# An S5 scan and a Mish layer on one core: both rotation products in one instruction, two reordered steps, one snapshot on VectorE, a shorter quarter-wise stage

## The chip, the cores and the metric

One core of a Trainium2 chip runs the whole kernel. The metric is the device time of one execution in microseconds (us); the runs shown are three executions of the kernel before, and their median is the time to be compared. TensorE does the matrix products, VectorE and ScalarE the elementwise work, GpSimd and SyncE mostly issue DMAs. Each engine works through its own queue in order; semaphores order the engines among each other.

## The reference

x has 2048 rows of 1024 (one batch). Types are bf16.

```
xn  = (x - mean) / sqrt(var + 1e-5)                       # per row
A:  Lam_bar = exp(dt * Lam);  B_bar = ((Lam_bar - 1) / Lam) * (B_re + i B_im)
    Bu = xn @ B_bar^T                                      # 2048 x 1024, complex
    h[t] = Lam_bar * h[t-1] + Bu[t]                        # along the rows
    A = 2 * Re(h @ (C_re + i C_im)^T) + xn * Dskip
B:  g = xn @ w1 + b1                                       # 1024 -> 3584
    B = (g * tanh(softplus(g))) @ w2                       # Mish, 3584 -> 1024
out = x + A + B
```

## The kernel before

The 2048 rows are worked on in four blocks of 512, counted from 0 as the variable `blk` does. Each block has the same stages on TensorE: the w1 product (Mish follows on ScalarE), the B product (the two parts of Bu), the w2 product, and the C product, which adds to the same eight PSUM banks as w2's; bank u holds quarter u // 2 of the block's rows and half u % 2 of the columns. `finish` then adds a quarter's two banks to x on VectorE (L1525) and ScalarE's queue stores the sum.

**The scan.** The complex recurrence is turned into two real ones: `recur` runs a real scan for each part (L1354, part "A") and rotates by tables of sine and cosine before and behind it. A rotation ("turn") takes the two parts of one row of 128 states, multiplies both by one table and then both by the other (two products into `mt`), and then forms a sum and a difference of those. It stands at three places: in `project_in` (block 0, read from PSUM), in `rotate_in` (before the scan of blocks 1 to 3) and in part "B" of `recur` (behind the scan). Eight rows j make the states; `hT` holds them, and later the C product's operands.

**Products with fewer multiplications.** From block 1 on the B product, and in blocks 2 and 3 w1's too, are done by a Strassen-Winograd scheme: seven products (numbered 1 to 7) of half size, whose PSUM banks are chained. In `w_product` a quad (letters p, q, s, w, x, y, z) opens bank X with product 1 and adds 6, 7 and 4 to it one after the other; bank Y holds product 2, bank Z products 5 and 3. Between two that chain on one bank, `w_evacuate` reads what is there: after 1, 5 and 6 a "snapshot" to SBUF (`snap`, L1004 on ScalarE or L1007 on VectorE, two instructions each), after 2, 3 and 7 a "join" of a bank and a snapshot (L1021, VectorE), after 4 a plain copy. So product 7 waits for the snapshot behind 6, and product 4 for the join behind 7.

**The order** is written out by hand in strings: `STEPS` for block 2, `LAST` for block 3. In them `p1` is product 1 of quad p with its evacuation, `a`..`d` are the B product's pairs, `r3` is rotate_in of row 3, `u0` the opening products of w2 on bank 0 (`open_unit`, the first six tiles f, from three ring slots), `g2` a Mish over a group of tiles (ScalarE), `h8` a scaling of a w2 row (ScalarE; each fourth also issues three stores on GpSimd's queue), `k0` one pending VectorE step (a sum of weights, L1134 or L1189, and a store on GpSimd's queue), `M1` a load on ScalarE's queue, `A0` and `B0` parts "A" and "B" of the scan of row 0, `S0` a few small VectorE instructions. What stands left to right is the order of each engine's own queue.

**Weights** stream through a ring of seven slots of 512 KB. SyncE issues the load of a slot as soon as TensorE has told that the slot's last user is done (`item_done`); the same SyncE queue carries the transposing DMAs of the next block's `xnT`.

**The tail.** In `tail` the last `njt` rows of the C product are done quarter by quarter (row j, part ci, then the quarter's two banks), so that `finish` of one quarter runs beside the next one's products; the other rows are done for all eight banks. `njt` is 1 in block 0 and 3 in blocks 1 to 3. The slots of the quarter-wise rows are given back behind the last quarter.

Of the kernel before, what the change touches and what calls it, by code (L numbers as in the profile page):

```python
# [5 lines left out]
ALU = mybir.AluOpType  # L6
# [3 lines left out]
P = 128  # L10
# [153 lines left out]
def build_kernel(nc, A_x, A_Lambda_re, A_Lambda_im, A_B_re, A_B_im, A_C_re, A_C_im,  # L164
# [5 lines left out]
    TB = 512  # L170
    NB = S // TB
# [14 lines left out]
             " d4 u6 r2 u4 n0 r3 r4 k0 k0 r5 k0 k0 n1 r6 r7")  # L186
    STEPS = ("p1 p5 p2 q1 q5 k0 k0 p6 q2 s1 k0 p7 s5 p3 k0 q6 s2 k0 p4 q7 k0 q3 k0 s6 q4 k0 m3 k0 g0 a2 a1 k0 s7 s3 k0 b2 b1 k0 s4 g1 m2 a5 "
            "b5 a6 b6 a3 b3 a7 b7 c2 d2 a4 b4 c5 c1 d5 d1 h12 r0 c6 c3 h13 d6 d3 h14 c7 h15 w1 d7 r1 w5 w2 l0 c4 d4 w6 x1 x5 x2 k0 w7 k0 w3 r2 "
            "x6 w4 y1 y5 y2 k0 k0 x7 x3 y6 A0 x4 z1 z5 g2 h8 h9 h10 M1 z2 B0 y7 h11 y3 z6 y4 u0 z7 u2 r7 z3 u1 z4 u7 r3 g3 r4 r6 r5")
    LAST = ("p1 p5 p2 q1 q5 p6 S0 q2 s1 p7 s5 p3 q6 s2 M4 p4 q7 q3 k0 k0 s6 q4 g0 a2 a1 k0 s7 k0 s3 m6 b2 b1 s4 G1 G0 g1 a5 G3 b5 G2 a6 b6 "  # L190
# [11 lines left out]
    VE = Queue(nc, "ve")  # L202
    AC = Queue(nc, "ac")
# [3 lines left out]
    def sb(name, shape, dtype):  # L207
        return nc.alloc_sbuf_tensor(name, shape, dtype)
# [17 lines left out]
    hT = sb("hT", [P, 2, NJ, TB], bf16)  # L226
    b_hT = [[Buf("hT%d_%d" % (ci, j)) for j in range(NJ)] for ci in range(2)]
# [3 lines left out]
    tab = sb("tab", [P, 2, NJ, TB], bf16)  # L231
    b_tab = [Buf("tab%d" % j) for j in range(NJ)]
# [6 lines left out]
    mt = sb("mt", [P, 2, 2, TB], bf16)  # L239
    b_m = [Buf("m%d" % i) for i in range(2)]  # L240
# [29 lines left out]
    def cj(n, j):  # L270
        return cs[:, CN.index(n), j:j + 1]

    ps = nc.alloc_psum_tensor("ps", [P, 8, TB], f32)
    b_ps = [Buf("ps%d" % i) for i in range(8)]
# [7 lines left out]
    hT16 = nc.alloc_sbuf_tensor_at("hT16", [P, 2, NJ, TB], f16, offset=base_h)  # L282
# [19 lines left out]
    def wsm(n, lo, hi):  # L302
        return cs[:, CN.index("den") + n, lo:hi]
# [71 lines left out]
    vop, aop, pop = VE.op, AC.op, PO.op  # L375
# [221 lines left out]
    def b1(f):  # L597
        return par[:, 3 * NJ + f:3 * NJ + f + 1]
# [88 lines left out]
    for f in range(4):  # L687
        first_raw(f, 0, NK // 2)
    PE.op(lambda e: e.transpose(ps16(6)[:, 0:NST], st[:, :], ident[0:NST, 0:NST]),
          reads=[b_st, b_ident], writes=[b_ps[6]])  # L690
# [184 lines left out]
    def banks_of(j):  # L875
        return 2 * ((j + 2) % 4)

    def rotate_in(j):
        for s in range(2):
            vop(lambda e, s=s: e.tensor_tensor(  # L880
                mt[:, s, :, :], hT16[:, :, j, :], tab[:, s, j, :].unsqueeze(1).to_broadcast([P, 2, TB]), op=ALU.mult),
                reads=[b_hT[0][j], b_hT[1][j], b_tab[j]], writes=[b_m[s]])
        vop(lambda e: e.tensor_tensor(hT[:, 0, j, :], mt[:, 0, 0, :], mt[:, 1, 1, :], op=ALU.add),
            reads=b_m, writes=[b_hT[0][j]])
        vop(lambda e: e.tensor_tensor(hT[:, 1, j, :], mt[:, 0, 1, :], mt[:, 1, 0, :], op=ALU.subtract),
            reads=b_m, writes=[b_hT[1][j]])
# [73 lines left out]
    def w_out(i, ci):  # L960
        f0 = 4 * i + 2 * ci
        return f0, *places(SPLIT[0], f0, 2)
# [27 lines left out]
    def w_evacuate(blk, i, n, keep):  # L990
        X, Y, Z = W_BANKS[i]
        at = REAL[i]
        ig = wsm(3, at, at + 1)
        b_ig = b_wsm[3][at]

        def bank(b):
            return ps[:, b, :].rearrange("p (j t) -> p j t", j=2)

        def whole(dst, b_dst, b, ci, queue):
            f0 = 4 * at + 2 * ci  # L1000
            for j in range(2):
                o, p = dst[:, j, :], ps[:, b, j * TH:(j + 1) * TH]
                if queue is AC:
                    aop(lambda e, o=o, p=p, j=j: e.activation(o, p, AF.Identity, scale=ig, bias=b1(f0 + j)),  # L1004
                        reads=[b_ps[b], b_par, b_ig], writes=b_dst)
                else:
                    vop(lambda e, o=o, p=p, j=j: e.tensor_scalar(o, p, ig, b1(f0 + j), op0=ALU.mult, op1=ALU.add),  # L1007
                        reads=[b_ps[b], b_par, b_ig], writes=b_dst)

        def snap(b, ci, queue):  # L1010
            k = free_snaps.pop(0)
            dst = snaps[:, 2 * k:2 * k + 2, D - TH:D]
            whole(dst, [b_snap[k]], b, ci, queue)
            return dst, k

        def join(b, kept, ci, th):
            src, k = kept
            free_snaps.append(k)
            f0, dst, b_dst = w_out(i, ci)
            dst = dst[:, :, th * TH:(th + 1) * TH]  # L1020
            vop(lambda e: e.scalar_tensor_tensor(out=dst, in0=bank(b), scalar=ig, in1=src, op0=ALU.mult, op1=ALU.add),  # L1021
                reads=[b_ps[b], b_snap[k], b_ig], writes=b_dst)

        if n == 1:
            keep["w", i, "a"] = snap(X, 0, AC)
        if n == 2:
            join(Y, keep["w", i, "a"], 0, 0)
        if n == 5:
            keep["w", i, "e"] = snap(Z, 1, AC)
        if n == 6:  # L1030
            keep["w", i, "v"] = snap(X, 0, VE if i == 6 else AC)
        if n == 3:
            join(Z, keep["w", i, "v"], 0, 1)
        if n == 7:
            join(X, keep["w", i, "e"], 1, 1)
        if n == 4:
            f0, dst, b_dst = w_out(i, 1)
            whole(dst[:, :, 0:TH], b_dst, X, 1, AC if i in (0, 1, 3, 4) else VE)
# [289 lines left out]
    def project_in():  # L1328
        for j in range(NJ):
            if j:  # L1330
                row_sizes(0, j - 1)
            bank = banks_of(j)
            for ci in range(2):
                for k in range(NK):
                    PE.mm(lambda e, j=j, ci=ci, k=k, bank=bank: e.matmul(  # L1335
                        ps[:, bank + ci, :], lhsT=BT[:, ci, j, k, :], rhs=xnT[:, k, :], start=k == 0, stop=k == NK - 1),
                        reads=[b_BT[j]] + b_xnT, writes=[b_ps[bank + ci]], first=k == 0, last=k == NK - 1)
            u = ps[:, bank:bank + 2, :]
            for s in range(2):
                vop(lambda e, s=s, u=u, j=j: e.tensor_tensor(  # L1340
                    mt[:, s, :, :], u, tab[:, s, j, :].unsqueeze(1).to_broadcast([P, 2, TB]), op=ALU.mult),
                    reads=[b_ps[bank], b_ps[bank + 1], b_tab[j]], writes=[b_m[s]])
            vop(lambda e, j=j: e.tensor_tensor(hT[:, 0, j, :], mt[:, 0, 0, :], mt[:, 1, 1, :], op=ALU.add),
                reads=b_m, writes=[b_hT[0][j]])
            vop(lambda e, j=j: e.tensor_tensor(hT[:, 1, j, :], mt[:, 0, 1, :], mt[:, 1, 0, :], op=ALU.subtract),
                reads=b_m, writes=[b_hT[1][j]])
            if j < 7:
                transpose_C(2 * j + 2)
                transpose_C(2 * j + 3)

    def recur(blk, j, parts="AB"):
        for ci in range(2 if "A" in parts else 0):
            init = 0.0 if blk == 0 else qi[:, ci, j:j + 1]
            vop(lambda e, ci=ci, init=init: e.tensor_tensor_scan(  # L1354
                out=hT[:, ci, j, :], data0=cj("r", j).to_broadcast([P, TB]), data1=hT[:, ci, j, :], initial=init,
                op0=ALU.mult, op1=ALU.add),
                reads=[b_hT[ci][j], b_cs["r"]] + ([b_qi] if blk else []), writes=[b_hT[ci][j]])
        if "B" not in parts:
            return
        for s in range(2):  # L1360
            vop(lambda e, s=s: e.tensor_tensor(  # L1361
                mt[:, s, :, :], hT[:, :, j, :], tab[:, s, j, :].unsqueeze(1).to_broadcast([P, 2, TB]), op=ALU.mult),
                reads=[b_hT[0][j], b_hT[1][j], b_tab[j]], writes=[b_m[s]])
        vop(lambda e: e.tensor_tensor(hT[:, 0, j, :], mt[:, 0, 0, :], mt[:, 1, 1, :], op=ALU.subtract),
            reads=b_m, writes=[b_hT[0][j]])
        vop(lambda e: e.tensor_tensor(hT[:, 1, j, :], mt[:, 0, 1, :], mt[:, 1, 0, :], op=ALU.add),
            reads=b_m, writes=[b_hT[1][j]])
        if blk == NB - 1:
            aop(lambda e: e.activation(hT[:, :, j, :], hT[:, :, j, :], AF.Copy, scale=wz[:, 2:3]),
                reads=[b_hT[0][j], b_hT[1][j], b_wz[2]], writes=[b_hT[0][j], b_hT[1][j]])  # L1370
# [17 lines left out]
    def tail(blk, base):  # L1388
# [38 lines left out]
                                     start=st_, stop=last),  # L1427
                  reads=[b_hT[ci][j], b_c], writes=[b_ps[bank]], first=st_, last=last)

        njt = 1 if blk == 0 else 3  # L1430

        X, Y, Z, W = (0, 2), (4, 6), (5, 7), (1, 3)
        BANKS = {1: X, 6: X, 4: X, 2: Y, 5: Z, 3: Z, 7: W}
# [72 lines left out]
        i = blk % 2  # L1506
# [22 lines left out]
        if ends:  # L1529
            for m, q0, h in ((0, 0, 0), (1, 0, 1), (2, 2, 0), (3, 2, 1)):  # L1530
# [3 lines left out]
                    reads=[b_KS[m]] + b_x, writes=[b_KS[m]])  # L1534
            tmp, b_tmp = KS[:, 3, 1, :], b_KS[3]
            vop(lambda e: e.scalar_tensor_tensor(out=tmp, in0=ps[:, 7, :], scalar=wz[:, 3:4], in1=tmp, op0=ALU.mult, op1=ALU.add),
                reads=[b_ps[7], b_tmp, b_wz[3]], writes=[b_tmp])
# [7 lines left out]
        if ends:  # L1545

            for h in range(2):
                lo = TB + 256 * h
                for j in range(NJ - njt, NJ):
# [5 lines left out]
                    reads=[b_ps[h], b_tmp, b_wz[3]], writes=[b_end[h]])  # L1555
# [102 lines left out]
    for blk in range(NB):  # L1658
# [70 lines left out]
        for j in range(NJ):  # L1729
# [8 lines left out]
            if blk in SPLIT:  # L1738
# [29 lines left out]
                if j == 6 and not near:  # L1768
                    vop(lambda e: e.tensor_tensor(KS[:, 1, :, :], KS[:, 1, :, :], KS[:, 3, :, :], op=ALU.add),
                        reads=[b_KS[1], b_KS[3]], writes=[b_KS[1]])  # L1770
# [39 lines left out]
        if blk == FAST - 1:  # L1810
# [3 lines left out]
                reads=[b_qi] + b_ss, writes=[b_qi])  # L1814
# [43 lines left out]
```

## Time and profile before

| what | us |
|---|---|
| median of three runs | 596.78 |
| the three runs | 596.63, 596.78, 598.31 |
| span of the profiled execution (its own time; the page has no other) | 596.5 |
| TensorE busy | 589.6 |
| VectorE, ScalarE, GpSimd busy | 499.8, 380.5, 166.4 |

The profile is of one execution. A span runs from the first instruction to the last. A row of the timeline gives start, duration, engine, line of the kernel, operation, tiles and shapes, how many instructions were merged into the row, and in brackets how long the engine sat idle before it and what ended that. L12 is line 12 of the kernel. "PEld" is TensorE's weight load, "SPq" and "ACTq" are DMA issues on a queue. A matmul's end is modelled: rows of TensorE overlap by about 0.17 us. The granted clock of TensorE is 1.000 over the whole span.

### The profile page before, as it was taken

What the parts mean: (1) busy time and instruction counts of PE and PEld (TensorE: products, weight loads), DVE (VectorE), ACT (ScalarE), POOL (GpSimd) and SP (SyncE); (2) the same over time, 40 slices, a digit from 0 to 9 for tenths busy, and PEclk for the clock granted to TensorE, in tenths of its full rate; (3) what the DMA queues carried; (4) which work ended last, traced back from release to release, by engine and by line L of the source; (5) the groups of instructions that cost most, each with busy time, mean ns of one, the idle gap of its engine ahead of it and who ended that gap; (6) DMA issues with size and microseconds to landing.
All of it is one profiled execution on the core that took longest, in us unless ns stands there. A gap on an engine that the chain in (4) does not pass through costs nothing. (4 is left out here: it accounts for less than half of the span.)

```text
span 596.5 us, 9558 instructions
## 1 busy us (share of the span) xinstructions
PE 589.6 (99%) x3555; PEld 345.0 (58%) x3555; DVE 499.8 (84%) x799; ACT 380.5 (64%) x512; POOL 166.4 (28%) x223
## 2 busy tenths in 40 slices
PE   8999999999999999999999999999999999999998
PEld 7644444444444487444458888544446788854444
DVE  6998899999789758999947867898498578789997
ACT  4749986589497526943537477798342798892320
POOL 2899300221246534130212321144210133100000
DMA  9999995992899964799679939999996966988831
GB/s 252 283 264 287 215 198 167 274 352 77 260 315 334 367 240 156 258 309 218 218 268 391 398 119 368 334 319 271 290 298 238 393 225 225 334 321 328 285 127 70
DMA packets 115975, 158.72 MB, mean 266 GB/s; under 512 B 55578, under 2 KB 70554, under 8 KB 115930
## 3 DMA queue, kind: packets, MB, share of 16 engines
q1 hardware_dynamic: 96960, 101.27, 56.6%
q0 software_dynamic: 14192, 46.42, 22.8%
q10 hardware_dynamic: 4778, 10.44, 4.9%
q8 instruction: 28, 0.46, 0.3%
q14 instruction: 17, 0.14, 0.1%
HBM read 111.95 MB, written 34.08 MB: 245 GB/s over the span
## 5 line engine op out<-in xcount | busy, mean ns | idle before, releaser
L1395 PE MATMUL ps<-ring,act 128*128 128x512 bf16 x672 | 146.4, 379 | 0.0
L1395 PEld LDWEIGHTS ps<-ring,act 128*128 128x128 bf16 x672 | 65.7, 98 | 77.9 <-DMA ring<-in_B_w_dram 0.4
L841 PE MATMUL ps<-xnT,ring 128*128 128x512 bf16 x392 | 84.9, 379 | 0.0
L1395 PE MATMUL ps<-ring,hT 128*128 128x512 bf16 x370 | 80.3, 379 | 0.0
L1004 ACT ACTIVATE snaps<-ps,par,cs 128x256 f32<-128x256 f32 x80 | 43.3, 563 | 41.8 <-DVE xx L1525 29.1
L841 PEld LDWEIGHTS ps<-xnT,ring 128*128 128x128 bf16 x392 | 38.3, 98 | 46.1
L1161 POOL DMA_DIRECT2D w2d<-hb x42 | 30.0, 717 | 120.6 <-DVE hb L1189 69.9
L1395 PEld LDWEIGHTS ps<-ring,hT 128*128 128x128 bf16 x370 | 36.2, 98 | 43.6
L984 PE MATMUL ps<-TT,ring 128*128 128x256 f16 x448 | 56.3, 273 | 2.9 <-ACT snaps L1004 1.7
L1354 DVE TENSOR_TENSOR_SCAN hT<-cs,qi,hT 128x512 bf16<-128x512 f32 x48 | 58.9, 1268 | 0.0
L1021 DVE SCALAR_TENSOR_TENSOR act<-ps,cs,snaps 128x512 bf16<-128x512 f32 x42 | 31.2, 748 | 23.8 <-PE ps L984 21.2
L984 PEld LDWEIGHTS ps<-TT,ring 128*128 128x128 f16 (+1 forms) x448 | 43.4, 98 | 10.1 <-issue 2.7
L849 ACT ACTIVATE act<-ps,par 128x512 bf16<-128x512 f32 (+1 forms) x56 | 34.1, 666 | 18.8 <-PE ps L841 17.0
L1113 POOL DMA_DIRECT2D wsd<-hb x42 | 22.9, 546 | 73.1 <-DVE hb L1134 42.8
L984 PE MATMUL ps<-xnT,ring 128*128 128x256 bf16 x336 | 42.9, 273 | 0.0
L1361 DVE TENSOR_TENSOR mt<-hT,tab 128x1024 bf16<-128x1024 bf16 x64 | 41.4, 688 | 1.0
L984 PEld LDWEIGHTS ps<-xnT,ring 128*128 128x128 bf16 (+1 forms) x336 | 32.8, 98 | 4.6
L1119 ACT ACTIVATE hb<-hb,cs 128x2048 bf16<-128x2048 bf16 x12 | 23.2, 1992 | 16.3 <-DVE cs L1108 16.3
L939 DVE TENSOR_TENSOR hT<-ps,snaps 128x512 f16<-128x512 f32 x36 | 24.4, 689 | 10.5 <-ACT snaps L931 7.0
L880 DVE TENSOR_TENSOR mt<-hT,tab 128x1024 bf16<-128x1024 f16 x48 | 30.9, 685 | 0.3
L864 ACT ACTIVATE act<-act 128x4096 bf16<-128x4096 bf16 (+2 forms) x8 | 25.5, 3185 | 8.1 <-DVE act L1007 8.1
L1335 PE MATMUL ps<-xnT,BT 128*128 128x512 bf16 x128 | 27.8, 379 | 0.0
(225 smaller groups left out, 1029.1 us busy)
## 6 DMA issues: line engine op xcount, KB each, us to landing
ring<-in_B_w_dram SPq DMA_DIRECT2D x70, 512.0 KB, 5.4
ring<-wsd SPq DMA_DIRECT2D x98, 256.0 KB, 6.0
ring<-ctd SPq DMA_DIRECT2D x24, 512.0 KB, 4.7
ring<-w2d SPq DMA_DIRECT2D x24, 512.0 KB, 4.7
wsd<-hb POOLq DMA_DIRECT2D x42, 256.0 KB, 5.5
w2d<-hb POOLq DMA_DIRECT2D x42, 256.0 KB, 5.3
hb<-in_B_w_dram POOLq DMA_DIRECT2D x24, 256.0 KB, 5.1
ctd<-act ACTq DMA_DIRECT2D x8, 512.0 KB, 6.9
```

The source lines that it names most:

```text
L841: PE.mm(lambda e, k=k, w=w: e.matmul(ps[:, bank, :], lhsT=w, rhs=xnT[:, k, :], start=k == 0, stop=k == NK - 1), reads=[b_ring[s]] + b_xnT, ...
L849: aop(lambda e: e.activation(at[0][:, ts], ps[:, bank, ts], AF.Mish, bias=b1(f)), reads=[b_ps[bank], b_par], writes=[at[1]])
L864: aop(lambda e: e.activation(t, t, AF.Mish), reads=b, writes=b)
L880: vop(lambda e, s=s: e.tensor_tensor(mt[:, s, :, :], hT16[:, :, j, :], tab[:, s, j, :].unsqueeze(1).to_broadcast([P, 2, TB]), op=ALU.mult) ...
L984: PE.mm(lambda e, w=w, x=x, o=o, begin=begin, end=end: e.matmul(ps[:, bank, o:o + TH], lhsT=w, rhs=x, start=opens and begin, stop=end, ski ...
L1004: aop(lambda e, o=o, p=p, j=j: e.activation(o, p, AF.Identity, scale=ig, bias=b1(f0 + j)), reads=[b_ps[b], b_par, b_ig], writes=b_dst)
L1021: vop(lambda e: e.scalar_tensor_tensor(out=dst, in0=bank(b), scalar=ig, in1=src, op0=ALU.mult, op1=ALU.add), reads=[b_ps[b], b_snap[k], b_ ...
L1161: PO.dma(lambda e: e.dma_start(w2d[at // 4][:, at % 4 * TB:(at % 4 + 2) * TB].rearrange("p (j t) -> p j t", j=2), t[:, :, d, :]), sem, rea ...
L1335: PE.mm(lambda e, j=j, ci=ci, k=k, bank=bank: e.matmul(ps[:, bank + ci, :], lhsT=BT[:, ci, j, k, :], rhs=xnT[:, k, :], start=k == 0, stop= ...
L1354: vop(lambda e, ci=ci, init=init: e.tensor_tensor_scan(out=hT[:, ci, j, :], data0=cj("r", j).to_broadcast([P, TB]), data1=hT[:, ci, j, :], ...
L1361: vop(lambda e, s=s: e.tensor_tensor(mt[:, s, :, :], hT[:, :, j, :], tab[:, s, j, :].unsqueeze(1).to_broadcast([P, 2, TB]), op=ALU.mult), ...
L1395: PE.mm(lambda e: e.matmul(ps[:, u, :], lhsT=lhsT, rhs=rhs, start=st_, stop=last, skip_group_check=blk == NB - 1), reads=reads, writes=[b_ ...
```

## The change

Four edits:

1. The two products of a rotation, so far two instructions of 1024 elements a partition, become one of 2048 (`turn`), at all three places. Both inputs are read with a repeated dimension: the operand once for each table, each table once for each part.
2. In `STEPS` (block 2) two places are reordered: `k0 k0 x7` becomes `k0 x7 k0`, and `z2 B0 y7 h11 y3 z6 y4` becomes `z2 y7 y3 z6 B0 h11 y4`. `LAST` stays.
3. The snapshot behind the first product of quad p (blocks 2 and 3) goes from ScalarE to VectorE.
4. `njt` becomes 1, 2, 2, 3 for blocks 0 to 3 (it was 1, 3, 3, 3).

```diff
@@ STEPS
-            "x6 w4 y1 y5 y2 k0 k0 x7 x3 y6 A0 x4 z1 z5 g2 h8 h9 h10 M1 z2 B0 y7 h11 y3 z6 y4 u0 z7 u2 r7 z3 u1 z4 u7 r3 g3 r4 r6 r5")
+            "x6 w4 y1 y5 y2 k0 x7 k0 x3 y6 A0 x4 z1 z5 g2 h8 h9 h10 M1 z2 y7 y3 z6 B0 h11 y4 u0 z7 u2 r7 z3 u1 z4 u7 r3 g3 r4 r6 r5")
@@ rotations
+    def turn(u, b_u, j):
+        vop(lambda e: e.tensor_tensor(
+            mt[:], u.unsqueeze(1).to_broadcast([P, 2, 2, TB]), tab[:, :, j, :].unsqueeze(2).to_broadcast([P, 2, 2, TB]),
+            op=ALU.mult), reads=b_u + [b_tab[j]], writes=b_m)
+
     def rotate_in(j):
-        for s in range(2):
-            vop(lambda e, s=s: e.tensor_tensor(
-                mt[:, s, :, :], hT16[:, :, j, :], tab[:, s, j, :].unsqueeze(1).to_broadcast([P, 2, TB]), op=ALU.mult),
-                reads=[b_hT[0][j], b_hT[1][j], b_tab[j]], writes=[b_m[s]])
+        turn(hT16[:, :, j, :], [b_hT[0][j], b_hT[1][j]], j)
...
@@ project_in
-            for s in range(2):
-                vop(lambda e, s=s, u=u, j=j: e.tensor_tensor(
-                    mt[:, s, :, :], u, tab[:, s, j, :].unsqueeze(1).to_broadcast([P, 2, TB]), op=ALU.mult),
-                    reads=[b_ps[bank], b_ps[bank + 1], b_tab[j]], writes=[b_m[s]])
+            turn(u, [b_ps[bank], b_ps[bank + 1]], j)
@@ recur
-        for s in range(2):
-            vop(lambda e, s=s: e.tensor_tensor(
-                mt[:, s, :, :], hT[:, :, j, :], tab[:, s, j, :].unsqueeze(1).to_broadcast([P, 2, TB]), op=ALU.mult),
-                reads=[b_hT[0][j], b_hT[1][j], b_tab[j]], writes=[b_m[s]])
+        turn(hT[:, :, j, :], [b_hT[0][j], b_hT[1][j]], j)
@@ w_evacuate
         if n == 1:
-            keep["w", i, "a"] = snap(X, 0, AC)
+            keep["w", i, "a"] = snap(X, 0, AC if i else VE)
@@ tail
-        njt = 1 if blk == 0 else 3
+        njt = 3 if blk == NB - 1 else min(blk + 1, 2)
```

## The prediction, made before the change was run

> **What bounds the kernel now.** I read the page's busy times first, then TensorE's waits, then the timeline around each of them, last the DMA answers for the same stretches.
>
> ```profile
> PE 589.6 (99%) x3555; PEld 345.0 (58%) x3555; DVE 499.8 (84%) x799; ACT 380.5 (64%) x512; POOL 166.4 (28%) x223
> ```
>
> TensorE is busy for all but 6.9 us of the 596.5, and the change takes no matmul away (below). All that it can win lies in TensorE's stalls; after the first 20 us the waits name these:
>
> ```profile
> PE ps L984 <- ACT snaps L1004: 1.7, 2, 1.5
> PE ps L984 <- DVE act L1021: 1.2, 2, 0.9
> ```
>
> A matmul's end is modelled, so I count stalls from start to start. Eight products of 256 columns take 0.873 us (366.16 to 367.03), six of 512 columns 1.31.
>
> ```profile
> 315.11 1.91 PE L984 MATMUL ps<-xnT,ring 128*128 128x256 bf16 x16
> 317.25 1.91 PE L984 MATMUL ps<-TT,ring 128*128 128x256 f16 x16 [0.24 <-ACT snaps L1004]
> ...
> 367.03 1.04 PE L984 MATMUL ps<-TT,ring 128*128 128x256 f16 x8
> 368.37 1.03 PE L984 MATMUL ps<-TT,ring 128*128 128x256 f16 x8 [0.30 <-DVE act L1021]
> ...
> 373.61 1.04 PE L984 MATMUL ps<-TT,ring 128*128 128x256 f16 x8
> 375.52 1.05 PE L984 MATMUL ps<-TT,ring 128*128 128x256 f16 x8 [0.88 <-DVE act L1021]
> 376.41 1.52 PE L1395 MATMUL ps<-ring,act 128*128 128x512 bf16 x6
> ...
> 458.56 2.12 PE L984 MATMUL ps<-TT,ring 128*128 128x256 f16 x16
> 460.57 1.91 PE L984 MATMUL ps<-xnT,ring 128*128 128x256 bf16 x16
> 463.94 1.91 PE L984 MATMUL ps<-TT,ring 128*128 128x256 f16 x16 [1.46 <-ACT snaps L1004]
> ```
>
> Counted along the order strings these are p7 of block 2, late by 0.39 (317.25 against 315.11 + 1.75); x4 by 0.47; y4 by 1.04; the first opening unit by 0.05; and in block 3 p6 by 0.26 and p7 by 1.62. Together 3.8 us: the most that the change can give.
>
> **The change part by part.** The snapshot of p1. In block 2 ScalarE, held by the last store of block 1, starts at 311.73 and makes six snapshots in a row; p7 needs the fifth (p6's), at 317.0. With p1's on VectorE (two of L1007's, 0.54 each, right after L1525 ends at 311.30, so done by 312.4) ScalarE has four ahead of p7 instead of five and is done about 1.1 earlier: the 0.39 goes. What queues behind it on VectorE is p2's join, now at 312.7 instead of 313.0, since it waited for ScalarE; nothing there is later.
>
> k0 x7 k0. x4 waits for x7's join, queued behind two steps L1189 (366.15 to 367.48). Behind one it can end at 367.5, under 367.9 where x4 wants to start: 0.47 goes. The second step, and with it its GpSimd store, is 0.75 later; ScalarE's load M1 waits for that store's landing, but M1's data are first used at 387.86.
>
> B0 behind y7, y3 and z6. y7's join sat behind B0's 2.0 us (372.73 to 374.72). In the new order y7's join, y3's join and z6's snapshot run when TensorE delivers them, B0 after those: y4 no longer waits. h11 passes no ScalarE instruction, because between its two places z6 and the joins are all VectorE's: nothing. B0's output is first read at 427.44, so it costs nothing.
>
> But what is late next after y4 is a transfer. The opening unit behind it reads three w2 slots, and the third one's load is issued when z2 ends:
>
> ```profile
> 372.10 0.37 SPq L436 DMA_DIRECT2D ring<-in_B_w_dram  x1
> ring<-in_B_w_dram SPq DMA_DIRECT2D x1, 512.0 KB, 5.2
> 377.32 0.11 PEld L1395 LDWEIGHTS ps<-ring,act 128*128 128x128 bf16 x2 [0.38 <-DMA ring<-in_B_w_dram]
> ```
>
> It lands at 377.3, exactly when used. Without stalls it would be wanted 1.9 earlier, at 375.4. Its issue moves by only 0.86 (the stalls before z2), and as the stage table shows the DMA engines at a share of 0.97 to 1.04 from 360 to 380, its landing may move by just the 0.39 by which the whole backlog starts earlier. I take 0.65, between the two: of 1.95 won so far, 0.65 survives.
>
> The merged products. Two products in SBUF take 1.28 a pair, one instruction of twice the size is in the trace:
>
> ```profile
> L1629 DVE TENSOR_TENSOR BT<-BT,act x8: 1215/1224/1225, 154.9 to 173.4; 128x2048 bf16<-128x2048 bf16 x8
> 379.51 1.28 DVE L880 TENSOR_TENSOR mt<-hT,tab 128x1024 bf16<-128x1024 f16 x2
> ```
>
> So 0.06 each, 64 times (8 of them from PSUM, where 2.36 for two gives, less one start of 0.15, some 2.29): 4 us of VectorE in all, of which TensorE sees only what shortens the chain into block 3. L1629 also repeats one operand, but this form repeats both; if the pair rate were lost, an instruction would cost about the 2.29 of the PSUM form, 1.0 more than now. I take 1.22, the nearest row. The Trainium skill, "VectorE: DVE Perf Modes", "What auto-detection actually checks", lists a step of plus or minus 1 on every 16-bit tensor as a condition of two results a cycle; read over the repeated dimension too, it speaks against this change (priced among the rivals), and L1629 says that a repeated row alone does not lose the rate.
>
> Two C rows quarter-wise. A block's C product stays 128 matmuls (8 rows x 2 x 8 either way). Row 5 is done whole, so row 7 is first needed 12 matmuls later (2.6 us). Its load, blocked behind the transposes on SP until 439.19, lands at 444.8 and is needed at 446.5 now (427.44 + 5 x 3.47 + 1.74), at 449.1 after: this covers the earlier TensorE, no more. The first finishes start 2.6, 1.7 and 0.9 later, the last as before (310.07): block 1's last add still ends at 311.3. The slot of row 5 comes free about 5 us sooner, into a stretch where the DMA moved 31 GB/s (450 to 455); p7's load gains, and no one waits for it. Nothing counted.
>
> Block 3's start is the largest item.
>
> ```profile
> 413.21 2.45 DVE L1354 TENSOR_TENSOR_SCAN hT<-cs,qi,hT 128x512 bf16<-128x512 f32 x2
> 425.51 2.94 DVE L1189 TENSOR_TENSOR act<-act 128x1024 f16<-128x1024 bf16 x4 [9.85 <-DMA w2d<-act]
> ...
> 453.28 4.61 DVE L1525 TENSOR_TENSOR xx<-ps,xx 128x1024 bf16<-128x1024 f32 x4
> 458.41 6.43 ACT L1004 ACTIVATE snaps<-ps,par,cs 128x256 f32<-128x256 f32 x12 [18.85 <-DVE xx L1525]
> ```
>
> VectorE idles 9.85 us for stores, during which all DMA nearly stands (48 GB/s in 417.5 to 420), then works without a gap from 425.51 to 457.89; ScalarE's store waits for that, its snapshots for the store, and p7 for the fifth, at 463.77. After the change the chain has four merged turns (0.25 less). If VectorE restarts at 425.5 again, it ends at 457.64 and ScalarE starts at 458.16; four snapshots of 1.06 and 0.04 between them end at 462.44, and p7 starts 0.17 later: 462.6, so 1.3 better than now. If the restart comes earlier by what was won before it (0.65 and six merged turns, 1.0), p7 could start at 461.65, close to TensorE's own 461.4: 2.3 better. I take a restart 0.3 earlier, near the lower end, since the stores leave at a time that DMA landings set: p7 at 462.3, **1.6 us** better, and this contains all that was won in block 2. Behind p7 nothing is nearer than the last block's row 7 (scaled at 582.9, needed at 566.5 + 17.4 + 1.7 = 585.6), and there VectorE gains ten merged turns itself: 1.6 stays to the end.
>
> The page gives no time of the profiled execution but its span, 596.5; the runs' median is 596.78. I take 1.6 from the span (594.9) and add the 0.3 between them: **595.1 us**.
>
> **The rivals.** (1) The pause of the DMA is an accident of the profiled execution. Then the timed runs before had no late VectorE chain, block 3 began like block 2 with 0.39 of stall, and only 0.65 + 0.39 is won: 595.7. For it: no other stretch of the trace has that idle time. Against: the median lies 0.3 above the profiled span, not below it.
> (2) The w2 slots are no limit, because everything in the DMA moves earlier, and the chain follows: 3.4 won, 593.4. Against it stands the backlog; the load would have to land 1.9 earlier.
> (3) Slower: the double repeat loses VectorE's pair rate, by the rule of the Trainium skill above, in a mechanism that rows price. In block 3 VectorE runs without a gap from 540.45 to the last turn, ten turns at +1.0: row 7 comes 10 later against 2.7 of margin, so +7, and about 4 more by the four turns behind 425.5, less what is won: about 606. It decides once an instruction is over 1.28 + 2.7/10 = 1.55.
> (4) The change doesn't do what it says: the order moves, but another VectorE or ScalarE item takes the waits' place in blocks 2 and 3, and under 0.6 remains: 596.5.
>
> **How the numbers follow.** Forecast, with a restart between fixed and fully shifted (594.5 to 595.5), 0.56; rival 1 0.21; rival 2 0.07; rival 3 0.06; rival 4 0.10. A measurement of this kernel tells 0.3% (1.8 us, 594.99) from no change. Faster by more than that are four tenths and a bit of the forecast's case (restarts earlier by 0.5 or more), 0.26, rival 2 and a few hundredths of rival 1 with a shorter tail: 0.36. Slower: rival 3 and a small share of rival 4, 0.08. The rest, 0.56, is within. The range 594.0 to 596.7 leaves out rivals 2 and 3 and the edges.
>
> **What would show it.** TensorE's waits on L1004 and L1021 gone in blocks 2 and 3 or under 0.3 each; in their place a wait of about 1.3 us on a w2 slot in the opening unit near 376; merged instructions at 1.22 us; VectorE's gap near 415 to 425, its end, and p7's start. Wrong would be: no DMA wait near 376; merged instructions over 1.5; a gap of VectorE under 4 us with p7's stall already gone; a new wait on VectorE.

## The result and the profile after

| | before | after |
|---|---|---|
| median of seven runs, us | 597.01 (596.63 to 598.31) | 595.53 (594.99 to 596.34) |
| ratio | 1 | 0.9971 [0.996, 0.9981] |
| span of the profiled execution, us | 596.5 | 593.9 (its own time: 595.5) |
| TensorE, VectorE, ScalarE busy, us | 589.6, 499.8, 380.5 | 587.5, 498.0, 378.7 |

By the medians the kernel became 1.5 us faster (0.25%), by the ratio 0.29%. The interval leaves out 1, so it is faster, and just inside the 0.3% that counted as no change. The forecast was 595.1. A ratio leaves disturbed executions out, and so can differ from the quotient of the medians.

TensorE's waits, the whole list after the change:

```profile
PE ps L614 <- DVE filler L446: 1.0, 1, 1.0
PE ps L1391 <- DMA ring<-in_B_w_dram: 0.7, 1, 0.7
PE ps L652 <- ACT xr L505: 0.2, 1, 0.2
```

The first and the last lie in the first 15 us. L986 (L984 before) is not in the list: the waits for snapshots and joins are gone, and one wait for a w2 slot is new. TensorE's timeline at the same three places (start, duration, instructions merged into the row, idle before and what ended it; the code has moved by two lines):

```profile
315.10 1.91 PE L986 MATMUL ps<-xnT,ring 128*128 128x256 bf16 x16
316.96 1.91 PE L986 MATMUL ps<-TT,ring 128*128 128x256 f16 x16
...
372.85 1.91 PE L986 MATMUL ps<-TT,ring 128*128 128x256 f16 x16
374.81 1.05 PE L1391 MATMUL ps<-ring,act 128*128 128x512 bf16 x3
376.56 0.60 PE L1391 MATMUL ps<-ring,act 128*128 128x512 bf16 x2 [0.70 <-DMA ring<-in_B_w_dram]
377.00 1.04 PE L986 MATMUL ps<-TT,ring 128*128 128x256 f16 x8
...
459.54 1.91 PE L986 MATMUL ps<-xnT,ring 128*128 128x256 bf16 x16
461.41 1.91 PE L986 MATMUL ps<-TT,ring 128*128 128x256 f16 x16
```

- **Start of block 2.** In both profiles the row ahead of p7 (q2 and s1) starts at 315.1, so here the two can be subtracted. p7 starts at 316.96 instead of 317.25; 0.12 of the 0.39 is left.
- **Middle of block 2.** z6 and y4 are one row without a gap. The opening unit behind them then waits for its w2 slots: 1.09 counted start to start (377.00 - 372.85 - 1.75 - 1.31). By the single instructions 0.23 of it is for the second slot and 0.86 for the third. z7 starts at 377.00 instead of 377.76, so 0.76 of the 1.95 survives.
- **Start of block 3.** p7 starts at 461.41 instead of 463.94, 0.12 behind its own pace (459.54 + 1.75). That is 2.5 us won, and the spans differ by 2.6: all of the gain stands at this point and stays to the end. The medians differ by 1.5 only, because the profiled execution of before was one of the slower of its seven (some 598.1 by its span, as worked out below).

The merged instruction in the page's groups (count, busy time, mean ns, idle before), then VectorE and ScalarE ahead of block 3's p7:

```profile
L879 DVE TENSOR_TENSOR mt<-hT,tab 128x2048 bf16<-128x2048 bf16 (+1 forms) x56 | 68.4, 1222 | 1.4
```

```profile
423.23 2.94 DVE L1191 TENSOR_TENSOR act<-act 128x1024 f16<-128x1024 bf16 x4 [8.82 <-DMA w2d<-act]
...
454.50 1.22 DVE L1521 TENSOR_TENSOR xx<-ps,xx 128x1024 bf16<-128x1024 f32 x1 [0.29 <-PE ps L1391]
455.64 1.11 DVE L1009 TENSOR_SCALAR snaps<-ps,cs,par 128x256 f32<-128x256 f32 x2
```

```profile
456.25 1.16 ACT L1006 ACTIVATE snaps<-ps,par,cs 128x256 f32<-128x256 f32 x2 [19.04 <-PE ps L986]
```

VectorE restarts at 423.23 instead of 425.51, its last add ends on TensorE's pace (released by `ps L1391`), it then takes p1's snapshot, and ScalarE's first snapshot is released by TensorE and no longer by the last store.

### The profile page after: what moved, and what is told of

It reads as the page before. It is cut to its first block, busy times and chain, and to the rows that moved or that the text cites. A ratio compares the mean times of both kernels' runs of the same rounds, so it can differ in the third digit from the quotient of the medians.

```text
span 593.9 us, 9456 instructions
## 1 busy us (share of the span) xinstructions
PE 587.5 (99%) x3514; PEld 346.2 (58%) x3555; DVE 498.0 (84%) x739; ACT 378.7 (64%) x508; POOL 166.2 (28%) x223
## 4 chain that ended last, share of the span: by engine, by line
PE 83%; DVE 9%; SPq 4%; DMA 2%; issue 1%; ACT 0%; DVEq 0%
PE ps L1391 31%; PE ps L841 14%; PE ps L986 14%; PE ps L916 12%; PE ps L1448 7%; SPq L824 4%; DVE hT L1353 3%; DVE CT L812 2%; DVE mt L879 2%; DVE CT L809 2%; PE ps L1337 1%; PE ps L652 1%; PE ps L661 1%; DMA ring<-in_B_w_dram 1%; DMA CT<-in_A_C_im_dram 1%
## 5 line engine op out<-in xcount | busy, mean ns | idle before, releaser
L1391 PE MATMUL ps<-ring,act 128*128 128x512 bf16 x657 | 145.6, 379 | 1.5 <-DMA ring<-in_B_w_dram 0.7
L1391 PEld LDWEIGHTS ps<-ring,act 128*128 128x128 bf16 x672 | 65.6, 98 | 79.1 <-DMA ring<-in_B_w_dram 1.7
L1391 PE MATMUL ps<-ring,hT 128*128 128x512 bf16 x362 | 79.9, 379 | 0.4
L1006 ACT ACTIVATE snaps<-ps,par,cs 128x256 f32<-128x256 f32 x76 | 41.5, 562 | 44.4 <-PE ps L986 39.2
L879 DVE TENSOR_TENSOR mt<-hT,tab 128x2048 bf16<-128x2048 bf16 (+1 forms) x56 | 68.4, 1222 | 1.4
L1391 PEld LDWEIGHTS ps<-ring,hT 128*128 128x128 bf16 x370 | 36.2, 98 | 43.6
L986 PE MATMUL ps<-TT,ring 128*128 128x256 f16 x448 | 55.8, 273 | 0.0
L986 PEld LDWEIGHTS ps<-TT,ring 128*128 128x128 f16 (+1 forms) x448 | 43.7, 98 | 6.3 <-issue 0.4
L986 PE MATMUL ps<-xnT,ring 128*128 128x256 bf16 x336 | 42.9, 273 | 0.0
L986 PEld LDWEIGHTS ps<-xnT,ring 128*128 128x128 bf16 (+1 forms) x336 | 32.9, 98 | 4.5
L1391 PE MATMUL ps<-CT,hT 128*128 128x512 bf16 x126 | 27.7, 379 | 0.1
```

The lines of the kernel that those rows point to most:

```text
L879: vop(lambda e: e.tensor_tensor(mt[:], u.unsqueeze(1).to_broadcast([P, 2, 2, TB]), tab[:, :, j, :].unsqueeze(2).to_broadcast([P, 2, 2, TB] ...
L986: PE.mm(lambda e, w=w, x=x, o=o, begin=begin, end=end: e.matmul(ps[:, bank, o:o + TH], lhsT=w, rhs=x, start=opens and begin, stop=end, ski ...
L1391: PE.mm(lambda e: e.matmul(ps[:, u, :], lhsT=lhsT, rhs=rhs, start=st_, stop=last, skip_group_check=blk == NB - 1), reads=reads, writes=[b_ ...
```

## The experiments

Each ratio is to runs of the kernel before on the same chip. The medians of before in the three groups of runs below were 598.14, 597.96 and 598.13. Stalls are counted start to start; each comes from one profiled execution.

My theory after the result had three parts: in block 2 a w2 slot's load takes the place of y4's wait; in block 3 the snapshot on VectorE shortens what lies between VectorE's late chain and p7 by one pair of snapshots; and that chain is late because of a pause of all DMA near 415 to 425, which something in the kernel causes. The rival was that the profiled execution of before had met an accident.

**e1: the changed kernel again.**

> The changed kernel once more, as the measure for the three beside it. Theory 1 (the win is the stalls of TensorE in the snapshots and joins): its profile has no wait on a snapshot or a join over 0.3 us, and one of about 1 us on a w2 slot near 375; ratio to before 0.997 to 0.998. Rival (the profiled execution of before was an odd one, and a usual one has hardly any stall at the start of block 3): the ratio is nearer to 0.998 to 0.999, and the profiles of both show the same p7.

Measured: 596.25, ratio 0.9965 [0.9953, 0.9976], span 594.7. VectorE here:

```profile
425.15 2.94 DVE L1191 TENSOR_TENSOR act<-act 128x1024 f16<-128x1024 bf16 x4 [10.07 <-DMA w2d<-act]
...
452.66 4.61 DVE L1521 TENSOR_TENSOR xx<-ps,xx 128x1024 bf16<-128x1024 f32 x4
457.19 1.12 DVE L1009 TENSOR_SCALAR snaps<-ps,cs,par 128x256 f32<-128x256 f32 x2
```

The restart is at 425.15, only 0.36 before that of the profiled execution of before, and the adds run back to back behind VectorE's chain. p7 nevertheless starts at 462.16, just 0.22 behind TensorE's own pace. The forecast for such a restart (0.3 earlier) was 462.3. That bears out the chain from the restart to p7.

Clock times of this profile can't be subtracted from those of the two before it, though. TensorE waits 1.45 for a weight load at 7.78, longer than in either of them, and the row ahead of block 2's p7 starts at 315.85, so 0.75 later; the spans of e1 and of the profile after differ by 0.8 (594.7 and 593.9). The opening unit waits 0.98 here.

**e2: the snapshot back on ScalarE.**

```diff
-            keep["w", i, "a"] = snap(X, 0, AC if i else VE)
+            keep["w", i, "a"] = snap(X, 0, AC)
```

> Edit 3 undone: the snapshot of p1 back on ScalarE in blocks 2 and 3. Theory 1 (five snapshots in a row behind the store are what p7 waits for): p7 of block 2 late by 0.3 to 0.4 again (ScalarE starts at 311.7, fifth snapshot ends at 317.0), p7 of block 3 late by 0.4 to 0.5 (ScalarE free at 456.2, five snapshots of 1.06, against 461.3); together 0.7 to 0.9 us slower than the changed kernel. Rival (at the start of block 3 it is VectorE's late chain alone that counts, and with that early the snapshot's place is indifferent): only block 2's 0.3 comes back, 0.3 us.

Measured: 597.53, ratio 0.998 [0.9965, 0.9994]. p7 of block 2 is late by 0.38 again, p7 of block 3 by 1.45, three times what I expected. ScalarE and TensorE:

```profile
458.35 6.43 ACT L1006 ACTIVATE snaps<-ps,par,cs 128x256 f32<-128x256 f32 x12 [18.55 <-PE ps L986]
```

```profile
463.87 1.91 PE L986 MATMUL ps<-TT,ring 128*128 128x256 f16 x16 [1.29 <-ACT snaps L1006]
```

p7 starts 1.71 later than in e1 (463.87 against 462.16). Of that 0.66 is VectorE's chain, which starts its adds at 453.32 instead of 452.66; the other 1.05 is one pair of snapshots more on ScalarE ahead of p7 (a snapshot takes 0.56). So behind a late VectorE chain the edit saves just what the prediction's sum of four snapshots instead of five gave it. By the two ratios the edit is worth 0.9 us (0.0015 of 598), but their intervals overlap. In this profile the opening unit also waits 1.99 for its slots, 0.9 more than in the profile after; that the edit does this is not shown.

**e3: the old order.** The two places of `STEPS` as in the kernel before.

```diff
-  ... k0 x7 k0 x3 y6 ... z2 y7 y3 z6 B0 h11 y4 u0 z7 ...
+  ... k0 k0 x7 x3 y6 ... z2 B0 y7 h11 y3 z6 y4 u0 z7 ...
```

> Edit 2 undone: the old order string of block 2. Theory 1 with the w2 slots as the limit behind y4: x4 late by 0.47 and y4 by 1.04 again, but the wait on the w2 slot (1.1 in the changed kernel) gone, so TensorE is only 0.4 to 0.5 later behind the opening unit and the kernel about 0.5 us slower than the changed one. Rival (the w2 wait is an effect of its own, not the other side of y4's): all 1.5 us come back.

Measured: 596.9, ratio 0.9981 [0.9969, 0.9993]. TensorE's two waits are back, and the one for the w2 slot is gone:

```profile
368.21 1.03 PE L986 MATMUL ps<-TT,ring 128*128 128x256 f16 x8 [0.30 <-DVE act L1023]
...
375.30 1.05 PE L986 MATMUL ps<-TT,ring 128*128 128x256 f16 x8 [0.81 <-DVE act L1023]
```

Start to start they are 0.47 and 0.98. So y4's 0.98 stands in the place of the slots' 1.09 (0.98 in e1), and of this edit about x4's 0.47 is left. The ratios (0.9981 against e1's 0.9965, 1.0 us) allow that, with intervals that overlap. The size of the slot wait is not firm: with the new order and the unit ahead of z7 it lies between 0.84 (e7) and 1.99 (e2).

**e4: two products again**, at all three places.

```diff
-        vop(lambda e: e.tensor_tensor(mt[:], ...[P, 2, 2, TB], op=ALU.mult), ...)
+        for s in range(2):
+            vop(lambda e, s=s, u=u, j=j: e.tensor_tensor(mt[:, s, :, :], u, ...[P, 2, TB], op=ALU.mult), ...)
```

> Edit 1 undone: two product instructions for each rotation. Theory 1 (0.06 us a rotation, felt only where VectorE's chain is what the next block waits for): VectorE's last add of block 2 later by ten rotations, 0.6, in the same places; TensorE's p7 of block 3 late by 0 to 0.4; under 0.4 us slower than the changed kernel, within the error of the time. Rival (VectorE, 84% busy, sets the pace of the last block): row 7 of block 3 later by 0.6 or more and the end with it, 0.6 us or more slower.

Measured: 596.3, ratio 0.9968 [0.9956, 0.9981], against e1's 0.9965. The only stall that is larger than in the profile after is that of the opening unit, 1.70 (0.85 each for the second and the third slot), and p7 of block 3 is late by 0.12 as there. The 4 us that merging takes off VectorE are worth nothing that the ratios can tell.

**e5: three rows quarter-wise again** in blocks 1 and 2.

```diff
-        njt = 3 if blk == NB - 1 else min(blk + 1, 2)
+        njt = 1 if blk == 0 else 3
```

> Edit 4 undone: three C rows quarter-wise in blocks 1 and 2. Theory 1 (a cover, not a gain): row 7 of block 2 is wanted 2.6 us sooner, at 445.7, its load lands at about 444.2 in the changed kernel, so no wait of TensorE or one under 0.3; the slot of row 5 free 5 us later; time as the changed kernel within 0.3 us. Rival (the early slot and the late rows are what brings the start of block 3 forward): waits of 0.5 us or more near 445 or behind 455.

Measured: 596.47, ratio 0.999 [0.9972, 1.0008]. I had expected no wait, or one under 0.3 us, and was wrong. A stall appears at a place where neither before nor after has one:

```profile
447.20 5.99 PE L1391 MATMUL ps<-ring,hT 128*128 128x512 bf16 x27 [0.85 <-DMA ring<-ctd]
```

Start to start it is 1.01 us, for the load of a C row. The prediction had seen this row land at 444.8 against a need at 446.5, and had called the later need "cover" for an earlier TensorE. Here TensorE wants the row at 446.2, only 0.3 earlier. What moved is the load:

```profile
440.66 1.37 SPq L436 DMA_DIRECT2D ring<-ctd  x1
ring<-ctd SPq DMA_DIRECT2D x1, 512.0 KB, 6.4
```

It is issued 1.5 later than in the profile of before (439.19), because the four transposes ahead of it on SyncE's queue take 9.30 instead of 7.06, and it lands 2.2 later, at 447.1. In the other profiles in which the pause comes ahead of it the row lands between 444.2 and 448.2, without the exchange at 439.6 (e7) and 441.1 (e11). So the cover is against a load whose time varies. For the time of the kernel the intervals of e5 and e1 overlap, the quotient of e5's medians is 0.9975, and the profiled execution (597.03) was above the median: the 1.0 belongs to this execution.

**e6: the opening unit one place later.** If the w2 slot is what is late, other work ahead of the unit should hide it.

```diff
-  ... h11 y4 u0 z7 u2 ...
+  ... h11 y4 z7 u0 u2 ...
```

> The changed kernel with one more swap in block 2's order: z7 ahead of the opening unit u0. Theory (the unit waits for the third w2 slot, landing at 376.5, and z7 fills the time): TensorE reaches the unit 0.87 later and its last two tiles at about 376.8, behind the landing; in place of 1.1 us of DMA wait z7 waits 0.3 to 0.5 for the snapshot of z6 (VectorE, until 375.0); 0.6 to 0.8 us faster than the changed kernel. Rival (slots land in the order and at the pace that the DMA sets, and the next one becomes late): the wait moves to another slot and nothing is won.

Measured: 595.92, ratio 0.9965 [0.9949, 0.9981]. The wait for the slot is gone, and z7 now waits 0.60 for z6's snapshot: 0.4 to 0.5 less stall, too little for these intervals.

**e7: the changed kernel without the exchange that comes ahead of the pause.** Ahead of the stores that VectorE waits for, GpSimd's queue carries a store of 128 numbers, one of 4 bytes from each partition, to DRAM (`qmd<-wz`, 0.5 KB, 12.7 us from issue to landing in the profile after).

```diff
-        PO.dma(lambda e: e.dma_start(qmd, wz[:, 0:1]), ...)
...
-        PO.dma(lambda e: e.dma_start(qmx[:, :], qmd.partition_broadcast(P)), ...)
+        vop(lambda e: e.tensor_copy(qmx[:, :], wz[:, 0:1].to_broadcast([P, P])), ...)
```

> The changed kernel without the exchange of the row bound between partitions: the store of 512 bytes and the load that spreads it are left out, and each partition uses its own bound (a copy on VectorE in their place). Theory (the small store, 128 pieces of 4 bytes, sets off the pause of all DMA traffic near 413 to 420): no such pause, VectorE's gap ahead of L1191 falls from 8.8 us to 2 to 4. Rival (the pause comes from other traffic there, such as stores of scaled w2 rows beside loads of C rows): pause and gap as before, 7 to 10 us.

Measured, one run: 595.16, span 593.6. The stretch from 415 to 420 in the stage table (length, busy times of PE, PEld, DVE, ACT, POOL with counts, clock, DMA share, GB/s), first of e1, then of e7, and VectorE's row in e7:

```profile
415.00:420.00 5.00, 4.95 (x24) 2.27 (x24) 0.08 (x1) 4.85 (x11) 0.00 (x0) 1.00 1.14 58
```

```profile
415.00:420.00 5.00, 5.00 (x25) 2.23 (x23) 2.27 (x4) 4.71 (x9) 1.37 (x2) 1.00 1.03 414
```

```profile
417.56 2.94 DVE L1191 TENSOR_TENSOR act<-act 128x1024 f16<-128x1024 bf16 x4 [3.52 <-DMA w2d<-act]
```

58 GB/s become 414, and VectorE's idle time falls from 10.07 to 3.52: the pause comes with the exchange. It is no accident of one execution.

**e8: the kernel before again.**

> The kernel before, a second profile. Theory (the profiled execution shown was one of the slower ones: the changed kernel's runs are 1.6 us above their spans, so 596.5 stands for about 598.1): the span comes out at 595.0 to 595.6 with p7 of block 3 late by 0.2 to 0.8 in place of 1.6, and the pause of the DMA shorter or VectorE's chain earlier. Rival (executions of before differ elsewhere, at the start or in the end): p7 late by 1.4 to 1.7 again.

Measured, one run: 596.58, span 595.0, so again the span and 1.6. The stalls of block 2 are the same to 0.02 (0.41, 0.47, 1.05). p7 of block 3 is late by 0.48 only, where the first profile had 1.62:

```profile
462.46 1.91 PE L984 MATMUL ps<-TT,ring 128*128 128x256 f16 x16 [0.32 <-ACT snaps L1004]
```

In the two profiles of before VectorE restarts 16.6 and 15.5 us after the issue of the 4-byte store (408.91 to 425.51, 408.63 to 424.12), in the two of after 15.4 and 16.8 (407.82 to 423.23, 408.36 to 425.15). In e2 to e6 it is 16.3 to 16.5. So the restart follows the store; the time between them differs by 1.4 us from execution to execution, for one and the same kernel. This execution is the fastest of the 28 of before in the last group of runs, whose median is 598.13; the first profile, at a span of 596.5 and so some 598.1, is nearer to the usual one.

**e9: the store later**, behind the stores that VectorE waits for and just ahead of the load that reads it.

```diff
-        PO.dma(lambda e: e.dma_start(qmd, wz[:, 0:1]), ...)     # ahead of the w2d stores
...
     def row_most():
+        PO.dma(lambda e: e.dma_start(qmd, wz[:, 0:1]), ...)
         PO.dma(lambda e: e.dma_start(qmx[:, :], qmd.partition_broadcast(P)), ...)
```

> The changed kernel with the small store of the row bound (128 pieces of 4 bytes) behind the stores that VectorE waits for, just ahead of the load that reads it. Theory (the store sets off the pause, whatever is queued behind it suffers): no pause near 415, one some 6 us long near 425 to 433; VectorE's gap ahead of L1191 3 to 4 us in place of 8.8 to 10; last add of block 2 released by TensorE and not by VectorE's chain. TensorE had at most 0.3 us of stall there, so the time is that of the changed kernel within 0.4 us. Rival (the pause belongs to that stretch of the kernel and leaving the exchange out only shifted the work): gap of 8 to 10 us again.

Measured: 595.73, ratio 0.9956 [0.994, 0.9972]. The pause moves with the store, to 425 to 435 (145 and 119 GB/s), where nobody waits for it, and VectorE's idle time is 2.87:

```profile
417.44 2.94 DVE L1191 TENSOR_TENSOR act<-act 128x1024 f16<-128x1024 bf16 x4 [2.87 <-ACT ln L566]
```

For TensorE little is left to win by it, since with the snapshot on VectorE the late chain held p7 for no more than 0.22 (e1).

**e10: e9 and e6 together.**

> The late store and z7 ahead of the opening unit together, as the version that should beat both kernels. Theory: stalls after the first 20 us are 0.1 for p7 in block 2, 0.5 to 0.7 for z7 in block 2 and 0.1 for p7 in block 3, so 0.8 in place of the changed kernel's 1.2 to 1.5; 0.3 to 0.7 us faster than it, a ratio to before of 0.996 to 0.997. Rival (the pause, moved, catches the transposes or the load of C row 7): a wait of TensorE between 427 and 454, and slower than the changed kernel.

Measured: 595.38, ratio 0.995 [0.9933, 0.9967], span 593.4. Behind the start only z7's wait for z6's snapshot is left in TensorE's waits (0.60 start to start):

```profile
PE ps L986 <- DVE snaps L1009: 0.4, 1, 0.4
```

Of the versions that ran more than once it has the lowest ratio. It beats the kernel before; against the changed kernel (0.9965 [0.9953, 0.9976] in another group of runs) the intervals overlap, so there its lead is not shown.

**e11: the kernel before without the exchange** (e7's edit).

> The kernel before without the exchange of the row bound (store and spreading load left out, each partition uses its own bound). Theory (the pause made VectorE late for block 3 and that made p7 late by 0.5 to 1.8 there): gap ahead of L1189 of 3 to 4 us, last add of block 2 released by TensorE, p7 of block 3 late by 0.4 as in block 2, the other stalls (0.4, 0.47, 1.05) as before; 0.3 to 1.5 us faster than the kernel before, by how late p7 is in the execution compared. Rival (p7's lateness is ScalarE's five snapshots alone): p7 late by 0.5 or more without the pause too.

Measured: 596.67, ratio 0.9975 [0.9956, 0.9995]. VectorE restarts at 418.87 behind 3.18 of idle time, and p7 of block 3 is late by 0.40, as in block 2; the other stalls stay (0.41, 0.46, 1.04). So by the ratio before loses 1.5 us (0.0025 of 598; the interval allows 0.3 to 2.6) to the pause, near the 1.2 between 1.62 and 0.40.

**e12: two stores that nobody reads**, added to the changed kernel in block 2: 128 pieces of 64 bytes near 336, 128 pieces of 4 bytes near 382.

```diff
+            if blk == SPLIT[0] and o == "b5":
+                PO.dma(lambda e: e.dma_start(probe64, par[:, 0:16]), ...)
+            if blk == SPLIT[0] and o == "r4":
+                PO.dma(lambda e: e.dma_start(probe4, par[:, 0:1]), ...)
```

> The changed kernel with two stores added in block 2 that nobody reads: 128 pieces of 64 bytes issued on GpSimd's queue near 336, and 128 pieces of 4 bytes near 382. Theory (pieces of 4 bytes to one run of 512 bytes in DRAM set off the pause, full 64 byte pieces do not): traffic of 250 GB/s or more near 336 to 346 as in the changed kernel, and a stretch of 5 us or more under 120 GB/s that begins 3 to 8 us after 382. Rival 1 (any small store does it): both places pause. Rival 2 (it is the place near 415 and its traffic): neither does.

Measured, one run: 599.89, span 598.3. The 4-byte store is issued at 381.61. Behind it, the stage table's two stretches from 385 to 395, where the profile after has 301 and 273 GB/s:

```profile
385.00:390.00 5.00, 5.00 (x25) 2.29 (x24) 4.83 (x9) 5.00 (x4) 0.29 (x1) 1.00 1.20 147
390.00:395.00 5.00, 5.00 (x25) 2.26 (x24) 4.93 (x6) 4.94 (x7) 3.26 (x5) 1.00 0.72 61
```

In steps of 1 us the traffic falls at 387, is 53 GB/s from 387 to 395, and comes back (268) as the store lands, 13.2 after its issue. Behind the 64-byte pieces, issued at 335.88, there is no such fall: 404 GB/s from 335 to 340 (408 in the profile after), 193 from 340 to 345 (195). But this says little. A pause that begins some 5 us after the issue would begin near 341, and from 342 on the changed kernel itself moves next to nothing (59 GB/s from 342 to 345, then 0). So the traffic that my expectation counted on is not there, and rival 1, that any small store does it, is not out.

The pause behind the 4-byte store comes on top of the one near 415, and VectorE's idle time near 415 grows to 14.21. Now even the snapshot on VectorE is no protection; TensorE waits for that chain:

```profile
PE ps L986 <- DVE xx L1528: 3.0, 1, 3.0
...
PE ps L986 <- ACT snaps L1006: 0.9, 1, 0.9
```

Start to start that is 3.20 + 1.11 = 4.3 us, and the run is 4.4 above the changed kernel's profiled one (595.5).

## Why the prediction was right, and where it was not

**What was right.** The snapshot and join waits went, the w2 slot came in their place, the merged product costs 1.222 us, and the gain is set at block 3's start. The forecast's w2 wait of about 1.3 measured 1.09. In the middle of block 2 0.65 was forecast to survive and 0.76 did; the slot landed 0.77 earlier, inside the bounds of 0.39 to 0.86. Rival 2 (the slots are no limit) is out by e3 and e6, rival 4 by the waits. Rival 3 is out by the group's 1222 ns: with both operands repeated an instruction of 2048 took 1.222 us, and the two of 1024 before it 1.28. By the Trainium skill's "VectorE: DVE Perf Modes", "What auto-detection actually checks", read over the repeated dimension, the rate would have halved. The trace does not bear out that reading.

**The restart of VectorE: "I take a restart 0.3 earlier".** Mis-sized. In the profile after it is 2.28 earlier, of which 1.09 is the store's earlier issue (408.91 to 407.82) and 1.19 the shorter time from the store to the restart in that execution. In e1 it is 0.36 earlier by the clock, but TensorE comes to block 2 0.74 later there than in the profile of before (315.85 against 315.11); counted from that row the restart is 1.10 earlier, the store 1.29 earlier and the time behind it 0.19 longer. That 0.36 looks like the forecast's 0.3 is luck. The bound "restarts at 425.5 again", because DMA landings set it, had no ground: the store that starts the pause moves with the kernel, by about the 1.0 of the prediction's upper bound. This is why 2.5 instead of 1.6 were won at p7 between the two profiles.

**"Add the 0.3 between" span and median.** Wrong. An execution's time is its span and 1.6, in all runs shown here (595.5 and 593.9, 596.25 and 594.7, 596.58 and 595.0). So the profiled execution of before took some 598.1, not 596.5 or 596.8. My 1.6 was taken off a 598.1, which would have given 596.5; 1.0 of missing gain (1.6 instead of 2.6) and 1.3 of missing time then nearly cancelled (595.1 against 595.53). So that the number is near is in part luck. (As written the sum gives 595.2, not 595.1. And the 2.29 of the PSUM form comes out of two times 1.22 less 0.15, not of 2.36 less 0.15; the merged instruction there measured 2.291.)

**Rival 1, "the pause is an accident".** It was half true, and the argument against it ("the median lies 0.3 above the profiled span") rested on the wrong 0.3. The pause is systematic (e7, e11, e12); its length is not (e8), and the stall it makes in before was 1.62 and 0.48 in two profiles.

**Two C rows: "nothing counted".** Right for the sum of the two profiles. The reason, "this covers the earlier TensorE, no more", was not: in e5 1.0 us is lost at 447 because the row's load comes 2.2 later than in the profile of before, while TensorE wants it only 0.3 earlier. What the edit is worth changes with that load. By the prediction's sum for the need (start of the C product + 5 x 3.47 + 1.74), three quarter-wise rows would have had it in time in the profile after (444.2 against 445.8), barely in e1 (446.3 against 446.4), and 1.3 late in e2 (448.2 against 446.9).

**Snapshot of p1.** In block 2 0.27 to 0.29 of the 0.39; its larger part is at block 3 (e2), as the prediction's sum of four snapshots instead of five had it.

**Do the stalls add up?** Where the pause plays no part for TensorE they can be compared over two kernels. e11 has 0.41 + 0.46 + 1.04 + 0.40 = 2.31 us of them, e10 0.13 + 0.60 + 0.12 = 0.85. The difference, 1.46, meets the difference of the ratios, 0.0025 x 598 = 1.5, though the intervals of the two are as wide as that. It supports the account; it does not prove it.

**What stays open.** Why the pause is longer in one execution than in another, what of the 4-byte store causes it (the size of its pieces, or that it is small at all), why the opening unit's slots and the C row land up to 2 us earlier or later in profiles of nearly the same kernel, and the 0.12 that p7 keeps in both blocks.

## What to carry to other kernels

Count the stalls of the engine that bounds the kernel start to start, and for each ask which transfer is late next: y4's wait of a microsecond was worth nothing, because loads landed just then. Before a stall is given a size from one profile, learn how a profiled span stands to its own run's time, and look at a second execution; here the largest stall was 1.62 in one and 0.48 in the other. Look at what was issued ahead of a stretch in which all DMA stands still: a small store can be the cause, and putting it behind what is waited for cost nothing here (e9).

## What the runs showed of the hardware

A store to DRAM of 128 pieces of 4 bytes, 512 bytes in all, holds up most of the core's DMA traffic for 6 to 8 us: 58 GB/s in e1 where e7 has 414, 61 in e12 where the changed kernel has 273. The traffic falls 5 to 7 us after the issue and is back about when the store lands, 11.4 (e10) to 13.3 us (e5) after it. The busy share of the DMA engines does not show the pause in stretches of 5 us (1.14 in e1's, 1.20 and 0.72 in e12's two); the moved bytes do.

Whether larger pieces do the same is open. The store of 128 pieces of 64 bytes, 8 KB, landed after 8.6 us, at a place with hardly any traffic to hold up. A hint for yes is in the kernel itself: a store of 128 pieces of 8 bytes (`scd<-sbf`), issued at 154.20 in the profile after, is followed by a fall from 394 GB/s (158 to 159) to 99 (161 to 163), and the traffic is back (375) when it lands, 8.8 after its issue. No run tested it.

VectorE and ScalarE took the same time for a snapshot of 128x256 from PSUM: 1.11 for two on VectorE, a mean of 562 ns on ScalarE. Moving it between the two was a question of the queues alone.
